# Two zero fills of a decode kernel, moved from SP's queue to four uneven DMAs of GpSimd

## The chip, the core and the metric

The kernel runs on one core of a Trainium2 chip. A core has five engines with instruction queues of their own: TensorE (PE) for matrix products, VectorE (DVE), ScalarE (ACT), GpSimd (POOL) and SyncE (SP), which here only issues transfers. Data move between HBM, the memory outside the core, and SBUF, the memory inside it with 128 partitions, by 16 DMA engines. SP, ACT and GpSimd each put their transfers on a queue of their own, and all queues are served by the same 16 DMA engines. One transfer is split over several of these engines; each of them adds one to a semaphore when its share has landed.

The metric is the device time of one execution in microseconds (us). Before the change the median of 3 runs is 809.98 us (809.77 to 810.98). The execution that was profiled took 810.97 us, and its span, from the first to the last instruction, is 808.1 us.

## The reference

One decode step of a layer, forward and backward: attention over the last W = 4096 of 32768 cached positions, then a gated feed-forward part, and the gradients of everything.

```python
x = A_x
h = x + _A_ref(_layernorm(x, axis=-1), A_k_cache, A_v_cache, A_wq, A_wo)
h2 = h + _B_ref(_layernorm(h, axis=-1), B_w_gate, B_w_up, B_w_down)
...
W = min(4096, max(256, Sk // 4))
k = jnp.repeat(k_cache[:, :, Sk - W:, :], rep, axis=1)
v = jnp.repeat(v_cache[:, :, Sk - W:, :], rep, axis=1)
...
_out, _vjp = jax.vjp(_f, A_x, A_k_cache, A_v_cache, A_wq, A_wo, B_w_gate, B_w_up, B_w_down)
_grads = _vjp(grad_out)
```

The gradients of the two caches have the caches' shape: 8 heads, 32768 positions, 256 values in bf16. Only the last 4096 positions of a head are touched by the step. The gradient of the other 28672 is zero, and these zeros have to be written: 2 caches x 8 heads x 14.7 MB, 235 MB in all.

## The kernel before

The kernel computes the eight groups of heads one after the other, first forwards (`scores` and `moments`, K and V of three to four groups held in SBUF), then the middle part (output projection, feed-forward part, its backward pass), then the eight groups backwards, each of which ends with two stores of 2 MB (L589), the last 4096 positions of its gradients. ACT's queue (`LD`) carries the loads after the first few, and all stores of results.

SP's queue (`ZQ`) carries the loads that come first: `x_bf` (L92), `wq` (L96, L97), K and V of the first groups, the gradient of the output and `wd` (L175 to L182). After these it does nothing but fill zeros, up to the end of the kernel. A fill writes one region of 2 MB: `zeros` is a tile of 128 partitions with ZW = 8192 bf16 values, 16 KB, in each. VectorE sets the first 5120 of its columns to zero and GpSimd the rest. The list `fills` holds the 112 regions in order: for each of the 8 heads 7 regions of `out_2` (the gradient of K) and 7 of `out_3` (of V). In memory a region is 128 rows of 16 KB that follow each other. One fill gives each of the 16 DMA engines 8 rows.

At most DEEP = 8 fills are in flight. Fill i counts on semaphore `zsem[i % 8]`, and SP waits for the fill eight places earlier before it issues the next (L195, in the profile under L196). After the last fill SP waits until all eight semaphores have their full count (L200 and L201). The fills are taken out of the planner's own bookkeeping, each with a semaphore of its own and in program order, and the last wait is declared as the fence for all of them. Nothing else in the kernel depends on a fill.

GpSimd has almost nothing to do: four constants, its part of `zeros` (L55) and two identity matrices. Its last instruction ends 4.2 us after the start. It issues no transfer.

Of the kernel before, what the change touches and what calls it, by code (L numbers as in the profile page):

```python
# [15 lines left out]
G = 8  # L16
Dh = 256
W = 4096
# [4 lines left out]
Sk = 32768  # L23
EPS = 1e-5
SCALE = 1.0 / 16.0
ZW = 8192
NZ = (Sk - W) * Dh // (128 * ZW)
ZM = 5120
DEEP = 8
# [5 lines left out]
def kernel(  # L35
        ctx, tc, A_x, A_k_cache, A_v_cache, A_wq, A_wo, B_x, B_w_gate, B_w_up, B_w_down, grad_out,
           out_0, out_1, out_2, out_3, out_4, out_5, out_6, out_7, out_8):
    nc = tc.nc
    LD = nc.scalar
    ZQ = nc.sync  # L40
# [12 lines left out]
    zeros = const.tile([128, ZW], bf16)  # L53
# [133 lines left out]
    fills = []  # L187
    for g in range(G):
        for o in (out_2, out_3):
            reg = o[0, g, 0:Sk - W, :].rearrange("s d -> (s d)").rearrange("(n p f) -> n p f", p=128, f=ZW)  # L190
            fills += [reg[i] for i in range(NZ)]
    zsem = [tc.alloc_semaphore(f"zsem{j}") for j in range(DEEP)]
    for i, reg in enumerate(fills):
        if i >= DEEP:
            tc.keep_in_program_order(ZQ.wait_ge(zsem[i % DEEP], 16 * (i // DEEP)))  # L195
        fill = ZQ.dma_start(out=reg, in_=zeros[:])  # L196
        tc.info.no_tile_sem_insts.add(fill.ins.name)
        tc.add_to_no_dep_group("fills", fill.ins)
        tc.keep_in_program_order(fill.then_inc(zsem[i % DEEP], 16))
    for j in range(DEEP):  # L200
        filled = tc.keep_in_program_order(ZQ.wait_ge(zsem[j], 16 * len(range(j, len(fills), DEEP))))  # L201
    tc.declare_fence(filled.ins, group="fills")
# [437 lines left out]
```

## Time and profile before

| what | value |
|---|---|
| median of 3 runs | 809.98 us |
| profiled execution, its time | 810.97 us |
| its span | 808.1 us |
| PE / DVE / ACT / POOL busy | 484.3 / 369.3 / 191.2 / 3.7 us |
| HBM read / written | 57.89 / 280.59 MB |
| fills on SP's queue | 112 x 2048 KB, 38.8 to 69.9 us from issue to landing, median 56.8 |
| stores of 2048 KB on ACT's queue (L589) | 16, median 17.4 us to landing |
| first fill issued | 17.9 us |
| ninth fill issued (the first that waits for a fill) | 58.06 us |
| last store of L589 issued | 727.6 us |
| last fill issued | 768.0 us |

Times within an execution are counted from the first instruction of the span. Views of the profile that are used below: the slices divide the span into 40 equal parts, and one digit is the busy share in tenths; a row of stretches begins with a stretch in us from the start and its length, then has the busy time and the number of instructions of PE, PEld, DVE, ACT and POOL, the clock granted to PE, the mean busy share of the 16 DMA engines and what they moved in GB/s; a line of the waits has the waiting engine with its line, what ended the wait, the us in total, the number of waits and the longest. A share slightly over 1 comes from packets that overlap by some ns.

### The profile page before, as it was taken

How to read it: one execution, taken by the hardware profiler on the slowest of the kernel's cores; microseconds unless marked ns; L12 is line 12 of the kernel's file. 1: busy time of each engine (PE TensorE's matmuls, PEld its weight loads, DVE VectorE, ACT ScalarE, POOL GpSimd, SP SyncE). 2: the span in 40 equal slices, each digit the busy share in tenths (PEclk: the TensorE clock that was granted, in tenths of full speed). 3: DMA queues.
4: the chain of work that ended last, by engine and by line, in shares of the span. 5: the costliest groups of instructions: out<-in, count | busy, mean ns of one | idle time of the engine just before them, and what ended most of it. 6: DMA issues, size and time to landing. Idle time of an engine off the chain costs nothing.

```text
span 808.1 us, 8346 instructions
## 1 busy us (share of the span) xinstructions
PE 484.3 (60%) x3128; PEld 252.7 (31%) x3151; DVE 369.3 (46%) x1152; ACT 191.2 (24%) x301; POOL 3.7 (0%) x9
## 2 busy tenths in 40 slices
PE   3799999999999955119326664533674664230000
PEld 2454545455455532108313322211231221000000
DVE  3279356455536417881336545258843444540000
ACT  1521331322330102001014243221232343330000
POOL 1000000000000000000000000000000000000000
PEclk9899999999999976559858557555555557555555
DMA  9999999999999999999999999999999999999994
GB/s 371 396 427 429 429 429 428 430 428 427 431 430 426 422 426 429 431 432 426 425 420 423 427 436 427 413 421 429 428 429 426 428 431 429 429 429 427 430 428 196
DMA packets 24942, 339.02 MB, mean 420 GB/s; under 512 B 2755, under 2 KB 3398, under 8 KB 4422
## 3 DMA queue, kind: packets, MB, share of 16 engines
q1 hardware_dynamic: 17842, 254.96, 74.4%
q10 hardware_dynamic: 7060, 83.53, 24.4%
q8 instruction: 24, 0.39, 0.2%
q14 instruction: 16, 0.13, 0.0%
HBM read 57.89 MB, written 280.59 MB: 419 GB/s over the span
## 4 chain that ended last, share of the span: by engine, by line
DMA 24%; PE 12%; DVE 11%; ACT 2%; issue 1%; DVEq 0%; ACTq 0%
DMA out_dram<-arena 24%; PE d_ps L579 4%; PE rows_ps L251 3%; PE tr_ps L248 3%; DVE arena L417 2%; DVE arena L587 2%; DVE arena L586 2%; DVE arena L472 1%; PE dqb_ps L458 1%; DVE arena L502 1%; DVE arena L595 1%; ACT arena L584 1%; ACT arena L539 1%; DVE arena L392 1%; ACT arena L583 0%
## 5 line engine op out<-in xcount | busy, mean ns | idle before, releaser
L579 PE MATMUL d_ps<-arena,rT 32*128 32x512 bf16 x256 | 59.5, 564 | 129.9 <-DVE arena L587 101.3
L303 DVE TENSOR_SCALAR arena<-arena,p_f 128x256 bf16<-128x256 bf16 x512 | 109.7, 281 | 53.8 <-PE M_ps L307 29.0
L248 PE MATMUL tr_ps<-ident_bf,arena 128*128 128x128 bf16 x1024 | 102.5, 254 | 29.1 <-DVE arena L541 25.4
L307 PE MATMUL M_ps<-arena 128*128 128x512 bf16 x489 | 118.4, 380 | 1.4 <-issue 0.6
L248 PEld LDWEIGHTS <-arena 128*128 128x128 bf16 x1024 | 74.5, 113 | 90.7 <-issue 88.6
L251 PE MATMUL rows_ps<-arena,vpad 128*16 128x512 bf16 x256 | 96.0, 470 | 6.0 <-ACT arena L265 2.8
L265 ACT COPY arena<-tr_ps 128x1024 bf16<-128x1024 bf16 x64 | 61.7, 1015 | 119.1 <-PE tr_ps L248 119.1
L587 DVE CAST arena<-d_ps 128x512 bf16<-128x512 f32 x64 | 43.5, 680 | 56.2 <-DMA out_dram<-arena 56.2
L583 ACT CAST arena<-d_ps 128x512 bf16<-128x512 f32 x64 | 37.7, 588 | 126.1 <-PE d_ps L579 122.2
L579 PEld LDWEIGHTS <-rT 32*128 32x128 bf16 x256 | 12.4, 98 | 165.2 <-issue 83.5
L307 PEld LDWEIGHTS <-arena 128*128 128x128 bf16 x512 | 46.4, 98 | 52.3 <-issue 6.3
L586 DVE CAST arena<-d_ps 128x512 bf16<-128x512 f32 x64 | 44.0, 688 | 37.4 <-PE d_ps L579 37.3
L311 PE MATMUL ok_ps<-arena 128*16 128x256 bf16 x512 | 59.3, 273 | 1.1 <-DVE arena L292 0.9
L584 ACT CAST arena<-d_ps 128x512 bf16<-128x512 f32 x64 | 38.1, 595 | 64.4 <-DMA out_dram<-arena 64.4
L311 PEld LDWEIGHTS <-arena 128*16 128x16 bf16 x512 | 44.5, 90 | 14.7 <-issue 4.5
L539 ACT COPY arena<-tr_ps 128x1024 bf16<-128x1024 bf16 x32 | 32.8, 1026 | 16.0 <-PE tr_ps L248 11.9
L251 PEld LDWEIGHTS <-vpad 128*16 128x16 bf16 x256 | 17.8, 91 | 44.1 <-issue 37.4
L541 DVE COPY arena<-tr_ps 128x1024 bf16<-128x1024 bf16 x32 | 21.9, 685 | 13.5 <-PE tr_ps L248 12.7
L463 ACT ACTIVATE arena<-dqb_ps 128x512 bf16<-128x512 f32 x8 | 4.8, 597 | 79.9 <-PE dqb_ps L461 55.0
L458 PE MATMUL dqb_ps<-arena,doT_f 128*128 128x256 f32 x64 | 19.5, 435 | 4.7 <-ACT arena L463 4.7
L417 DVE CUSTOM_DVE_ANT_0 arena<-arena,dh_bc 128x448 bf16<-128x448 bf16 x32 | 20.0, 624 | 1.1
L253 DVE COPY arena<-rows_ps 16x512 f32<-16x512 f32 x16 | 10.8, 675 | 19.9 <-PE rows_ps L251 19.7
(182 smaller groups left out, 318.1 us busy)
## 6 DMA issues: line engine op xcount, KB each, us to landing
out_dram<-zeros SPq DMA_DIRECT2D x112, 2048.0 KB, 56.8
out_dram<-arena ACTq DMA_DIRECT2D x16, 2048.0 KB, 17.4
arena<-in_A_v_cache_dram ACTq DMA_DIRECT2D x8, 2048.0 KB, 14.8
arena<-in_A_k_cache_dram ACTq DMA_DIRECT2D x5, 2048.0 KB, 21.2
arena<-in_A_v_cache_dram SPq DMA_DIRECT2D x4, 2048.0 KB, 30.5
arena<-in_A_k_cache_dram SPq DMA_DIRECT2D x3, 2048.0 KB, 26.1
arena<-in_A_wo_dram ACTq DMA_DIRECT2D x1, 3584.0 KB, 19.3
arena<-in_A_wq_dram SPq DMA_DIRECT2D x1, 3072.0 KB, 10.2
```

What stands on the lines that cost most here:

```text
L248: nc.tensor.transpose(tr_ps[:, dh, i, :], X_sb[:, 4 * q + i, dh * 128:(dh + 1) * 128], ident_bf[:])
L251: nc.tensor.matmul(rows_ps[:], lhsT=pad[:, dh, 16 * q:16 * q + 16], rhs=XT[:, dh].rearrange("p t k -> p (t k)"), start=(q == 0 and dh == 0 ...
L265: sT_ps = dots(K_slot[g % 3], KT_slot, vpad[g % 2], rows1, ps_c, "cols", lambda q, XT, ps: nc.scalar.copy(out=XT, in_=ps))
L303: nc.vector.tensor_scalar(out=pK[:, i, hh, :], in0=K_sb[:, t, :], scalar1=p_f[:, 8 * i + c, hh:hh + 1], scalar2=None, op0=ALU.mult)
L307: nc.tensor.matmul(M_ps[:, vh, :], lhsT=V_sb[:, t, vh * 128:(vh + 1) * 128], rhs=pK[:, i, :, :].rearrange("p h d -> p (h d)"), start=(t == ...
L311: nc.tensor.matmul(ok_ps[:, k, :], lhsT=ppad[g % 2][:, 8 * (t % 4) + t // 4, :], rhs=X_sb[:, t, :], start=(g == 0 and k == 0 and t == 0), ...
L539: nc.scalar.copy(out=XT, in_=ps)
L579: nc.tensor.matmul(d_ps[:, qi].rearrange("p w d -> p (w d)"), lhsT=rT[32 * q:32 * (q + 1), :], rhs=RB_[32 * q:32 * (q + 1), l, :], start=T ...
L583: nc.scalar.copy(out=stV[:, t:t + 2, :], in_=d_ps[:, :, 0, :])
L584: nc.scalar.copy(out=stK[:, t:t + 2, :], in_=d_ps[:, :, 1, :])
L586: nc.vector.tensor_copy(out=stV[:, t:t + 2, :], in_=d_ps[:, :, 0, :])
L587: nc.vector.tensor_copy(out=stK[:, t:t + 2, :], in_=d_ps[:, :, 1, :])
```

## The change

The last two regions of `out_3` of the last head are taken from the list of SP's fills. They lie behind each other in memory: 256 rows of 16 KB, `last`. GpSimd writes them in four DMAs, each with a semaphore of its own, after it has waited for the first of SP's fills:

- rows 0 to 67, 4 times 17 rows, read from partitions 0, 4, 8 and 12 of `zeros`, each of them 17 times over
- row 68 without its last element, read from partition 16
- rows 69 to 119, 3 times 17 rows, read from partitions 20, 24 and 28
- rows 120 to 255, 8 times 17 rows, read from partitions 64, 68 and so on up to 92

The last element of row 68 is written by SP, as a DMA of one element ahead of its first fill. The row without it has 8191 elements, which is a prime. SP then issues 110 fills as before, and waits for the five new semaphores before it waits for the eight old ones. The helper `fill_with` holds the three lines that every fill had.

```diff
+    def fill_with(queue, dst, src, sem):
+        fill = queue.dma_start(out=dst, in_=src)
+        tc.info.no_tile_sem_insts.add(fill.ins.name)
+        tc.add_to_no_dep_group("fills", fill.ins)
+        tc.keep_in_program_order(fill.then_inc(sem, 16))
+
+    last = out_3[0, G - 1, 0:Sk - W, :].rearrange("s d -> (s d)").rearrange("(r f) -> r f", f=ZW)[(NZ - 2) * 128:NZ * 128]
+    tc.keep_in_program_order(nc.gpsimd.wait_ge(zsem[0], 16))
+    psem = []
+
+    def share(queue, dst, src):
+        psem.append(tc.alloc_semaphore(f"psem{len(psem)}"))
+        fill_with(queue, dst, src, psem[-1])
+
+    for r0, k, p0 in ((0, 4, 0), (68, 0, 16), (69, 3, 20), (120, 8, 64)):
+        if k:
+            share(nc.gpsimd, last[r0:r0 + 17 * k].rearrange("(k n) f -> k n f", n=17), zeros[p0:p0 + 4 * k:4].unsqueeze(1).to_broadcast([k, 17, ZW]))
+        else:
+            share(nc.gpsimd, last[r0:r0 + 1, 0:ZW - 1], zeros[p0:p0 + 1, 0:ZW - 1])
+    share(ZQ, last[68:69, ZW - 1:ZW], zeros[0:1, 0:1])
+
+    fills = fills[:-2]
     for i, reg in enumerate(fills):
         if i >= DEEP:
             tc.keep_in_program_order(ZQ.wait_ge(zsem[i % DEEP], 16 * (i // DEEP)))
-        fill = ZQ.dma_start(out=reg, in_=zeros[:])
-        tc.info.no_tile_sem_insts.add(fill.ins.name)
-        tc.add_to_no_dep_group("fills", fill.ins)
-        tc.keep_in_program_order(fill.then_inc(zsem[i % DEEP], 16))
+        fill_with(ZQ, reg, zeros[:], zsem[i % DEEP])
+    for sem in psem:
+        tc.keep_in_program_order(ZQ.wait_ge(sem, 16))
     for j in range(DEEP):
         filled = tc.keep_in_program_order(ZQ.wait_ge(zsem[j], 16 * len(range(j, len(fills), DEEP))))
```

## The prediction

> **What bounds the kernel now.** I read the page's slices first, then its queues, then stretches of the end, and last the packets of the end one by one.
>
> ```profile
> DMA  9999999999999999999999999999999999999994
> GB/s 371 396 427 429 429 429 428 430 428 427 431 430 426 422 426 429 431 432 426 425 420 423 427 436 427 413 421 429 428 429 426 428 431 429 429 429 427 430 428 196
> ...
> q1 hardware_dynamic: 17842, 254.96, 74.4%
> q10 hardware_dynamic: 7060, 83.53, 24.4%
> ```
>
> The sixteen DMA engines are busy from the first slice to the last but one, at about 428 GB/s, and 339 MB have to pass. q1 is SP's queue (all zero fills and the first loads), q10 is ACT's. So the time is what the DMA engines have to carry, and no compute engine sets it. Only the last slice (20.2 us long) is half empty. Stretches of it, with the DMA share in the last column but one:
>
> ```profile
> 727.00:751.00 24.00, 0.00 (x0) 0.00 (x0) 0.21 (x1) 0.60 (x2) 0.00 (x0) 0.50 1.01 428
> ...
> 768.00:792.00 24.00, 0.00 (x0) 0.00 (x0) 0.00 (x0) 0.00 (x0) 0.00 (x0) 0.50 1.01 429
> 792.00:794.00 2.00, 0.00 (x0) 0.00 (x0) 0.00 (x0) 0.00 (x0) 0.00 (x0) 0.50 0.88 377
> 794.00:796.00 2.00, 0.00 (x0) 0.00 (x0) 0.00 (x0) 0.00 (x0) 0.00 (x0) 0.50 0.69 295
> 796.00:798.00 2.00, 0.00 (x0) 0.00 (x0) 0.00 (x0) 0.00 (x0) 0.00 (x0) 0.50 0.56 238
> 798.00:800.00 2.00, 0.00 (x0) 0.00 (x0) 0.00 (x0) 0.00 (x0) 0.00 (x0) 0.50 0.23 98
> 800.00:802.00 2.00, 0.00 (x0) 0.00 (x0) 0.00 (x0) 0.00 (x0) 0.00 (x0) 0.50 0.08 33
> 802.00:804.00 2.00, 0.00 (x0) 0.00 (x0) 0.00 (x0) 0.00 (x0) 0.00 (x0) 0.50 0.08 33
> 804.00:806.00 2.00, 0.00 (x0) 0.00 (x0) 0.00 (x0) 0.00 (x0) 0.00 (x0) 0.50 0.06 25
> ```
>
> From 728 us on nothing computes; until 792 all engines copy zeros; then they run out one after the other. A share of 0.06 is one engine of sixteen: from 801.5 us on a single engine works. The view of the DMA queues from there:
>
> ```profile
> DMA packets 10, 0.13 MB, mean 20 GB/s; under 512 B 2, under 2 KB 2, under 8 KB 2
> ```
>
> Eight packets of 16 KB and two of 4 bytes (the count on the semaphore): this engine's whole last fill, while the other fifteen have nothing. SP waits for it:
>
> ```profile
> SPq L201 <- DMA out_dram<-zeros: 38.4, 4, 23.9
> ```
>
> The records of the packets (queue, start, length, size; no engine number) can be followed, since an engine starts a packet 3 to 4 ns before its last one ends. In the end the sixteen chains finish at 792.4, 793.2, 793.9, 794.9, 795.4, 795.4, 797.3, 797.6, 797.7, 797.9, 798.2, 799.1, 799.3, 799.9, 800.7 and **806.4 us**. Mean 797.5, median 797.6: one engine is 8.8 us late against the median and 5.7 against the next. In the same chains, where they can be followed, the late engine carries 9 of the 16 packets of 8 KB of the instruction queue q14 (0.31 us each, 2.8 us), and its 16 KB packets take 619 ns in the mean against 615 (4 ns by 1,152 packets, 4.6 us). I take both to come back in every execution, and the lateness as a property of one engine and not as chance.
>
> **The change, part by part.** The price of a row (16 KB) is the step between packets of the late engine in its last fill: 801.536 to 802.143, 0.607 us.
>
> *Taken off.* Two fills leave SP: 2 x 8 = 16 rows on each engine, 16 x 0.607 = 9.7 us on each.
>
> *Added, if the four parts fall as the change means them, on engines 0 to 3, 4, 5 to 7 and 8 to 15.* 68/4, 51/3 and 136/8 are 17 rows on fifteen engines, 10.3 us, and one row on engine 4, 0.6 us. Net: fifteen engines +0.61 us, engine 4 -15 x 0.607 = -9.1 us. If engine 4 is the late one, it ends at 806.4 - 9.1 = 797.3 us, and the end is set by the next: 800.7 + 0.6 = 801.3. **Gain 806.4 - 801.3 = 5.1 us.**
>
> *The price of a row issued by GpSimd* is not in the trace. Lower bound: 0.607, the row of SP's own; a 4 KB packet of the load of L97 steps by 0.153 to 0.155, four of them 0.61 to 0.62, so cutting the rows would cost nothing either. Upper bound: the 16 KB packets of the instruction queue q8, from another ring, at about 0.94 us in the records: 17 x (0.94 - 0.607) = 5.7 us on fifteen engines, which eats the gain (801.3 + 5.7 = 807.0, 0.6 later than before). It is a copy of zeros out of SBUF like SP's, so I take 0.607.
>
> *Which engine gets which rows* decides the sum, and no row of GpSimd's DMAs is there to read. [...]
>
> *Issue.* GpSimd's last instruction before the change ends at 4.2 us; its four DMAs hold up nobody behind them. They wait for the first fill's semaphore, which SP's ninth fill also waits for (issued at 58.06 us), so they start there and have until 801 to land. Should an issue take even tens of us, 740 us cover it.
>
> *SP's one-element DMA* stands before the first fill (17.9 us) and delays it and all behind it by one issue: 0.33 us (the median of L196's issues), or nothing if the loads still in the rings cover it. The stretch 20 to 30 us has a DMA share of 0.90, so some of the delay can become empty time: I take +0.2, bounds 0 and 0.33.
>
> *SP's four new waits and the fifth for the one element* stand after the last fill and before the eight old ones. The shares landed some 700 us earlier; behind them queue only those eight waits, of which the longest lasts 23.9 us today. Nothing.
>
> *Three rings in place of two from 58 us.* Until GpSimd's 17 rows are through (17 x 0.607 x 2 to 3 rings = 21 to 31 us) ACT's loads get a third of an engine and not half. The loads of K and V issued at 68.5 and 70.5 us land in 14.2 to 22.6 us today (all four from 60 to 110 us); by 3/2 that is 21 to 34, and the groups follow each other every 30 us, so PE may stall some 4 us once. What hides it: the last store is issued at 727.6 and landed by 751, and 55 us of nothing but fills follow. Without this cover it would cost these 4 us.
>
> *Sum:* -5.1 + 0.2 = **-4.9 us**. Against the profiled execution (span 808.1, its time 810.97) that is 806.1; the median of the runs is 809.98, 1.0 lower, so I put the forecast at **805.1 us**, -0.6%. Its own range goes from 803.4 (the next engine 1.7 us earlier than in this execution; the five before it lie within 2.5) to 807.0 (a third of the upper surcharge for GpSimd's rows, 1.9 us).
>
> **Rivals.** *The late engine is not the one relieved.* The records give no number. Against it: the relief, 9.7 us relative to the others, is the size of the lateness, 8.8; and the one-packet transfers of 896 bytes lie on chains that are not late, so at least the engine that takes single packets is not meant. For it: nothing else in the trace marks engine 4. Then the late engine gets its extra row: +0.6 + 0.2, 809.98 + 0.8 = 810.8 us. [...] No run here has shown a number so far.
>
> *The parts are not what they say.* If each is spread over all sixteen engines, or the row of 8,191 elements is cut, nobody is relieved: 809.98 + 0.2 = 810.2 us.
>
> *The parts pile up on the first engines, slower.* If every part starts at engine 0 with one partition to an engine, engine 0 gets 17 + 1 + 17 + 17 = 52 rows in place of 16. It becomes the end as soon as its surplus passes its lead: (806.4 - 797.5)/0.607 = 15 rows; here it is 36, 21.9 us. From the mean 797.5 that ends at 819.4, 13.0 us later than now: 809.98 + 13.0 + 0.2 = **823.2 us**. For it: the diff names partitions and counts, no engine, and a DMA that is told nothing else may start at the first. Against it: nothing in the trace. [...]
>
> *The row is as dear as q8's packets:* the end is at 807.0, 0.6 later than now: 809.98 + 0.6 + 0.2 = 810.8 us.
>
> **How the numbers follow.** Forecast 0.60; late engine elsewhere 0.18; spread evenly 0.05; dear rows 0.03; piled up 0.14. The first is faster, the next three lie within 0.2% (1.6 us, about what a measurement of this kernel can tell from no change), the last is slower: faster 0.60, same 0.26, slower 0.14. The range reaches from 803.4 to 811.2, over forecast and the cases of no change, and leaves the pile-up out.
>
> **What would show it.** Right: a queue of GpSimd with 256 packets of 16 KB, 4.19 MB; the stretch with a share of 0.06 gone and the share falling from full to nothing within about 9 us and not 14; SP's longest wait behind the last fill shorter by about 5 us; 1.01 up to about 793. Wrong: a lone engine that still copies a whole fill at the end (not the one relieved), one that copies for over 10 us alone (piled up), packets of GpSimd well over 0.62 us. The prediction fails above all if the number 4 is not the late engine's.

## The result and the profile after

The changed kernel takes 815.07 us (median of 5 runs, 813.7 to 817.01) against 809.98 us before (median of 5, 809.74 to 810.98): 0.6% slower, a ratio of 1.0062 with a 95% interval of [1.0045, 1.0079]. The forecast was 805.1 us, the range ended at 811.2. The profiled execution took 813.7 us with a span of 811.9.

The slices and the new queue on the page of the changed kernel:

```profile
DMA  9999999999999999999999999999999999999996
GB/s 369 398 427 428 395 354 396 430 424 429 424 431 427 416 424 429 434 429 430 427 420 427 425 430 429 415 418 429 432 428 425 429 432 427 434 428 430 430 428 265
...
q0 software_dynamic: 896, 4.20, 1.5%
```

q0 is GpSimd's queue: 256 packets of data, 4.20 MB as planned, and 640 packets of 4 bytes. The row of DMA digits shows nothing, but the rate falls to 395, 354 and 396 GB/s in the fifth to seventh slice, where 429, 429 and 428 stood. The same in stretches of 20 us (the last three columns are PE's clock, DMA share and GB/s):

```profile
60.00:80.00 20.00, 20.00 (x115) 9.90 (x114) 18.36 (x92) 3.00 (x4) 1.59 (x3) 1.00 1.01 426
80.00:100.00 20.00, 19.87 (x146) 10.54 (x145) 6.49 (x31) 7.51 (x12) 0.00 (x0) 1.00 1.01 402
100.00:120.00 20.00, 16.98 (x97) 8.72 (x95) 10.60 (x50) 2.61 (x3) 0.00 (x0) 0.83 1.00 352
120.00:140.00 20.00, 19.87 (x152) 11.33 (x151) 7.68 (x35) 6.73 (x12) 0.00 (x0) 1.00 1.01 400
```

A share of 1.00 at 352 GB/s means that the engines are always at work on a packet and that the packets take longer. The whole stretch from 60 to 160 us, first in the kernel before and then in this one:

```profile
60.00:160.00 100.00, 98.75 (x656) 51.51 (x666) 57.06 (x269) 29.18 (x44) 0.00 (x0) 1.00 1.01 429
60.00:160.00 100.00, 96.59 (x627) 49.28 (x625) 54.29 (x253) 27.56 (x38) 1.59 (x3) 0.97 1.01 400
```

So 100 x 29/429 = 6.8 us of all engines is lost there. From 60 to 80 us, where the first of GpSimd's parts runs, the rate is 426 GB/s against 430 before; the loss comes with the later parts. One sign that the prediction had named as "wrong" is there: packets of GpSimd well over 0.62 us. Its rows take 764 ns in the mean. The end:

```profile
798.00:800.00 2.00, 0.00 (x0) 0.00 (x0) 0.00 (x0) 0.00 (x0) 0.00 (x0) 0.50 0.85 360
800.00:802.00 2.00, 0.00 (x0) 0.00 (x0) 0.00 (x0) 0.00 (x0) 0.00 (x0) 0.50 0.73 311
802.00:804.00 2.00, 0.00 (x0) 0.00 (x0) 0.00 (x0) 0.00 (x0) 0.00 (x0) 0.50 0.69 295
804.00:806.00 2.00, 0.00 (x0) 0.00 (x0) 0.00 (x0) 0.00 (x0) 0.00 (x0) 0.50 0.48 205
806.00:808.00 2.00, 0.00 (x0) 0.00 (x0) 0.00 (x0) 0.00 (x0) 0.00 (x0) 0.50 0.25 106
808.00:810.00 2.00, 0.00 (x0) 0.00 (x0) 0.00 (x0) 0.00 (x0) 0.00 (x0) 0.50 0.10 41
```

All engines end later: the share is under 0.5 from 804 us on, before from 798 on, and the last fill is complete at 810.1 us against 806.4. One sign that the prediction had named as "right" came true all the same, in SP's waits behind its last fill:

```profile
SPq L222 <- DMA out_dram<-zeros: 38.4, 5, 19.1
```

The longest is 4.8 us shorter (23.9 before). With 110 fills in place of 112 another fill is the first that is waited for; this number follows the order of the waits and says nothing of the late engine.

When the packets are followed from engine to engine as in the prediction, the row of 16,382 bytes (at 88.87 us, 1.16 us long) stands on an engine that has done its 17 rows of the *first* part. No engine has a single row alone, and one has none. So the theory for the experiments: the row took no engine of its own and did not move the place at which the next DMA starts. The three shares fell on engines 4 to 6 and the eight on 7 to 14, each one engine lower than meant. Then engine 4 has 17 rows and is not relieved. Engines are numbered here in the order in which GpSimd's DMAs take them; the trace has no numbers. The sources in the diff suppose that partition 0 goes with engine 0, 4 with engine 1 and so on to 28 with engine 7, and 64 to 92 with engines 8 to 15; these are called an engine's own partitions below. If SP's fills are split in this way, each of these eleven engines reads from the partitions that the engine above it reads in the fills. The rival: the parts lie where they should, and GpSimd's rows are dear by themselves.

### The profile page after: what moved, and what is told of

It reads as the page before. It is cut to its first block, busy times and chain, and to the rows that moved or that the text cites. A ratio compares the mean times of both kernels' runs of the same rounds, so it can differ in the third digit from the quotient of the medians.

```text
span 811.9 us, 8375 instructions
## 1 busy us (share of the span) xinstructions
PE 487.9 (60%) x3151; PEld 253.0 (31%) x3151; DVE 369.5 (46%) x1152; ACT 191.2 (24%) x301; POOL 6.5 (1%) x13
## 5 line engine op out<-in xcount | busy, mean ns | idle before, releaser
L328 PE MATMUL M_ps<-arena 128*128 128x512 bf16 x512 | 123.2, 385 | 0.0
L616 DVE CUSTOM_DVE_ANT_0 arena<-arena 128x4096 bf16<-128x4096 bf16 x3 | 13.3, 4421 | 14.9 <-DMA arena<-in_A_wq_dram 14.9
## 6 DMA issues: line engine op xcount, KB each, us to landing
arena<-in_A_v_cache_dram ACTq DMA_DIRECT2D x8, 2048.0 KB, 19.4
arena<-in_A_k_cache_dram ACTq DMA_DIRECT2D x5, 2048.0 KB, 23.3
arena<-in_A_wq_dram SPq DMA_DIRECT2D x1, 3072.0 KB, 10.5
```

The source lines that it names most:

```text
L328: nc.tensor.matmul(M_ps[:, vh, :], lhsT=V_sb[:, t, vh * 128:(vh + 1) * 128], rhs=pK[:, i, :, :].rearrange("p h d -> p (h d)"), start=(t == ...
```

## The experiments

All times are medians beside runs of the kernel before on the same chip, whose medians were 809.85 to 810.28 us.

**Sources moved to where the theory has the shares.** Only partitions change:

```diff
-    for r0, k, p0 in ((0, 4, 0), (68, 0, 16), (69, 3, 20), (120, 8, 64)):
+    for r0, k, p0 in ((0, 4, 0), (68, 0, 0), (69, 3, 16), (120, 8, 60)):
```

> The changed kernel with other source partitions for three of GpSimd's four DMAs, nothing else: the row of 8191 from partition 0, the three shares from 16, 20, 24, the eight shares from 60, 64, ... 88. [...] With these sources every engine reads its own: GpSimd's rows take 0.61 us, the stretch from 80 to 135 us keeps about 428 GB/s (changed kernel: 339 to 410), and the time is 810.6 to 811.0 us, since the late engine keeps one row more than before (+0.6). Rival (dear rows: GpSimd's rows slow everything whatever they read): about 815 us as in the changed kernel. [...]

Measured: 811.58 us (810.67 to 812.35, 11 runs), ratio 1.0015 [1.0007, 1.0024]: 3.5 us under the changed kernel, and still 0.6 over the 811.0 us expected at most. DMA queues in the changed kernel from 80 to 110 us (packets, MB, share of 16 engines' time):

```profile
q1 hardware_dynamic: 383, 5.57, 50.1%
q10 hardware_dynamic: 248, 3.54, 27.6%
q0 software_dynamic: 386, 2.29, 23.3%
```

and the same stretch with the sources moved:

```profile
q1 hardware_dynamic: 431, 6.24, 48.8%
q10 hardware_dynamic: 277, 4.01, 31.3%
q0 software_dynamic: 430, 2.59, 20.8%
```

23.3% of 480 us is 111.8 us for 2.29 MB, 140 rows: 0.80 us a row, the small packets included. With the sources moved it is 20.8%, 99.8 us for 158 rows, 0.63 us. SP's rows gain as well (0.71 to 0.62 us by the same sum). The same bytes to the same addresses by the same engines: where a row is *read* makes the difference. That it comes from two readers of the same partitions, and not from the distance, agrees with the changed kernel from 60 to 134 us, where the chains can be followed. Engine 15 has no row of GpSimd's, but engine 14 reads from its partitions, and its own 16 KB packets take 730 ns in the mean. Engines 0 to 3, whose partitions no other engine reads, have 618 to 624 ns. If the parts had lain where the change meant them, this edit would have put them wrong and made things worse.

**Aligned and turned, without the odd row.** Three parts of 4, 4 and 8 engines with 16 rows each, no relief; first from the partitions of their own engines, then each from those of the next:

```diff
-    for r0, k, p0 in ((0, 4, 0), (68, 0, 16), (69, 3, 20), (120, 8, 64)):
...
+    for r0, k, p0 in ((0, 4, 0), (64, 4, 16), (128, 8, 64)):    # aligned
+    for r0, k, p0 in ((0, 4, 4), (64, 4, 20), (128, 8, 68)):    # turned
+        share(nc.gpsimd, last[r0:r0 + 16 * k].rearrange("(k n) f -> k n f", n=16), zeros[p0:p0 + 4 * k - 3:4].unsqueeze(1).to_broadcast([k, 16, ZW]))
```

> The two fills by GpSimd in three even parts, 4, 4 and 8 engines with 16 rows each, read from partitions 0 to 12, 16 to 28 and 64 to 92, no one-row DMA: nobody is relieved. [...] Rival (dear rows): 6 us of all engines are lost again, about 815 to 816 us.

> [...] Rival (dear rows): the same time as the even kernel within 0.2%.

Measured: aligned 810.56 us (809.95 to 811.46, 11 runs), ratio 1.0005 [0.9996, 1.0013], just over the 809.9 to 810.5 us expected if nothing is lost; turned 819.52 us (817.14 to 821.22, 4 runs), 1.012 [1.0105, 1.0136], inside the 816 to 820 us expected if the partitions make the difference. The stretch from 60 to 160 us, aligned:

```profile
60.00:160.00 100.00, 99.61 (x672) 52.05 (x671) 57.06 (x269) 29.18 (x44) 1.06 (x2) 1.00 1.01 424
```

and turned:

```profile
60.00:160.00 100.00, 92.59 (x611) 48.08 (x609) 52.06 (x245) 26.72 (x38) 0.96 (x2) 0.95 1.00 396
```

So reading each share from the next engine's partitions costs 28 GB/s over 100 us, and 9 us in all. A row of GpSimd's took 0.78 us from 60 to 110 us, against 0.64 aligned, by the sum used above (20.7% and 18.2% of 800 us, for 3.48 and 3.74 MB, the small packets included). The fills of GpSimd by themselves cost about 1 us at most (the upper end of the aligned interval). The two runs agree with the assignment that the diff's sources suppose; no trace shows it directly.

**Engine 4 given almost nothing, first try.** Six DMAs of half rows; the three small ones have one piece to an engine. They are to leave engine 4 one row and give each of the others 17:

```diff
+    for k, n, p0 in ((4, 33, 0), (4, 1, 16), (8, 1, 64), (5, 1, 0), (3, 33, 20), (8, 33, 64)):
```

> [...] If engine 4 is the late one: 805.1 us, 0.6% faster. Theory (the late engine lies among engines 1 to 3, since in the changed kernel the chain with the instruction queue q14 carried rows of the first part): 810.6 to 811.0 us, the late engine has one row more. Dear rows: 815 us or more.

Measured: 813.66 us (813.43 to 815.51), ratio 1.0045 [1.0032, 1.0058]. None of the three numbers was met, for a reason that is itself an answer. In the chains, engines 0 to 3 have their 33 half rows and then three single ones: each DMA with one piece to an engine began at the first engine, and none moved the place for the next. So the large parts behind them fell on 4 to 6 and 7 to 14 again, with the source partitions of others, and the rate from 60 to 160 us was 404 GB/s.

**Which engine is late?** With 16 pieces of 512 bytes to an engine for the small parts the place does move, by the rates below. First engine 2 is left one row, then engine 3, and the others have 17:

```diff
+    for k, n, w, p0 in ((2, 33, 4096, 0), (6, 16, 256, 8), (8, 16, 256, 64), (3, 16, 256, 0), (5, 33, 4096, 12), (8, 33, 4096, 64)):    # engine 2
+    for k, n, w, p0 in ((3, 33, 4096, 0), (5, 16, 256, 12), (8, 16, 256, 64), (4, 16, 256, 0), (4, 33, 4096, 16), (8, 33, 4096, 64)):    # engine 3
```

> [...] If engine 2 is the late one the time is 805.1 to 806 us; if not, 810.6 to 811.2. [...]

> The same for engine 3: 3 engines with 33 half rows, 5 and 8 with pieces of 512 bytes, 4 with pieces, 4 and 8 with 33 half rows. [...] If neither this nor the kernel for engine 2 is faster and both are free of slow rows, engine 1 is left of the three, or the lateness does not belong to one engine.

Measured: 811.49 us (810.93 to 812.68), 1.0017 [1.0008, 1.0026], and 811.36 us (810.88 to 812.92), 1.0016 [1.0007, 1.0025], both 0.2 to 0.3 over the 810.6 to 811.2 us expected for "not the late one". From 60 to 160 us the rates are 422 and 423 GB/s, as in the kernels whose shares are read from their own engines' partitions (422 and 424). With engine 3 relieved the end is:

```profile
802.00:804.00 2.00, 0.00 (x0) 0.00 (x0) 0.00 (x0) 0.00 (x0) 0.00 (x0) 0.50 0.06 25
804.00:806.00 2.00, 0.00 (x0) 0.00 (x0) 0.00 (x0) 0.00 (x0) 0.00 (x0) 0.50 0.08 33
806.00:808.00 2.00, 0.00 (x0) 0.00 (x0) 0.00 (x0) 0.00 (x0) 0.00 (x0) 0.50 0.04 16
```

One engine still works alone for 5 us. And the engine that carries most of q14's packets is the one without rows here, and ended at 792.4 us: it is number 3, and not the late one.

Then a kernel, run once, whose fourteen parts make each engine known: eight pairs of engines, then groups of 3, 2, 3, 3, 2 and 3, each with 8 rows, issued after SP's 96th fill. For each part without rows for it an engine handles 9 small packets, and one behind each set of its own (1,760 in all, of the 2,016 packets of its queue). So the numbers of small packets before, between and behind an engine's two sets of rows tell which it is:

```diff
-    tc.keep_in_program_order(nc.gpsimd.wait_ge(zsem[0], 16))
+    tc.keep_in_program_order(nc.gpsimd.wait_ge(zsem[7], 16 * 12))
...
+    for k, n, p0 in ((2, 8, 0), (2, 8, 8), (2, 8, 16), (2, 8, 24), (2, 8, 64), (2, 8, 72), (2, 8, 80), (2, 8, 88), (3, 8, 0), (2, 8, 12), (3, 8, 20), (3, 8, 64), (2, 8, 76), (3, 8, 84)):
```

> A look, not a gain: which engine is the late one. Neither engine 2 nor engine 3 is, by the two kernels before: in both a lone engine still ended some 5 us behind the rest while the relieved one stopped early. [...] The place of an engine's rows among the counts on the semaphores tells its number, and from there to the end its packets can be followed without a gap. Theory (one and the same engine is late): the lone engine of the last 5 us is again there, at about 806 us, it is none of 2, 3 and 15, and it has 8 + 8 rows like all others. Rival (no engine is late as such; whichever has the last of the fills by chance): the lone engine is any, 3 among them. Time 809.9 to 810.6 us.

Measured: 811.56 us, 1.0 over the range. When the sixteen chains are followed back from their ends, the one that ends alone, at 807 us, has 18 small packets, 8 rows, 55 small packets, 8 rows and 37 small packets. That is engine 4: two parts before (18), six between (54 + 1), four behind (36 + 1). The chain with 18, 64 and 28, which is engine 5, ends at 799.9 us, and the one with 9, 64 and 37, engine 3, at 802.1 us. The late engine is number 4, as the change has it.

**Engine 4 relieved, and the change with its row altered.** The first of the two kernels leaves engine 4 16 KB, about one row, and gives each of the others 17.

```diff
+    for k, n, w, p0 in ((4, 33, 4096, 0), (4, 16, 256, 16), (8, 16, 256, 64), (5, 16, 256, 0), (3, 33, 4096, 20), (8, 33, 4096, 64)):
```

> The 4.19 MB in six DMAs of GpSimd, all of them with several pieces per engine, so that the place of the next engine moves on with each: 4 engines x 33 pieces of 8 KB, 4 x 16 pieces of 512 B, 8 x 16 of 512 B, 5 x 16 of 512 B, 3 x 33 of 8 KB, 8 x 33 of 8 KB. [...] Theory (the late engine is number 4, and what ate the gain was the row that took no engine of its own): the lone engine at the end is gone, the share falls from full to nothing within 9 us, and the time is 805.1 to 806.5 us (-5 us for the engine, up to +1 for what all kernels with DMAs of GpSimd lost). Rival (the late engine is another, or lateness follows the load rather than an engine): 810.6 to 811.8 us, with one engine that ends alone near 807. Rival (relief of one engine shows in the tail, but the DMAs of GpSimd cost what is won): lone end gone, 808 to 810 us.

```diff
-            share(nc.gpsimd, last[r0:r0 + 1, 0:ZW - 1], zeros[p0:p0 + 1, 0:ZW - 1])
-    share(ZQ, last[68:69, ZW - 1:ZW], zeros[0:1, 0:1])
+            share(nc.gpsimd, last[r0:r0 + 1, 0:17 * 481].rearrange("k (n f) -> k n f", n=17), zeros[p0:p0 + 1, 0:481].unsqueeze(1).to_broadcast([1, 17, 481]))
+    share(ZQ, last[68:69, 17 * 481:ZW], zeros[0:1, 17 * 481:ZW])
```

> The change with one thing altered: row 68 is written by GpSimd as 17 pieces of 481 elements from partition 16, where the change has one piece of 8,191 elements, and its last 15 elements (in place of one) by SP. [...] Rival (a DMA with one partition stays at the first engine whatever its pieces): the shares shift by one as in the change, rows of 0.73 to 0.87 us at 80 to 110 us, 813 to 815.5 us.

Measured: with engine 4 relieved 807.44 us (806.29 to 810.32, 12 runs), ratio 0.997 [0.9961, 0.9978], the first of the kernels faster than before; above the 805.1 to 806.5 of the theory, below its rivals' 808. The lone engine at the end is gone:

```profile
800.00:802.00 2.00, 0.00 (x0) 0.00 (x0) 0.00 (x0) 0.00 (x0) 0.00 (x0) 0.50 0.27 115
802.00:804.00 2.00, 0.00 (x0) 0.00 (x0) 0.00 (x0) 0.00 (x0) 0.00 (x0) 0.50 0.06 25
804.00:806.00 2.00, 0.00 (x0) 0.00 (x0) 0.00 (x0) 0.00 (x0) 0.00 (x0) 0.50 0.00 0
```

With the row in 17 pieces 813.79 us (813.4 to 816.32), 1.0053 [1.0041, 1.0066]: inside the 813 to 815.5 us of the rival. The 17 pieces of 962 bytes were spread, two each over eight engines (8 packets of 1,924 bytes) and one on a ninth (a packet of 966 bytes), and the place again did not move. So several pieces did not move it where all lie in one partition. The prediction's pile-up rival has every part start at engine 0; that held for the smallest of the change's parts alone.

**Engine 3 too, and later.** Five DMAs with larger pieces, which leave engine 4 half a row, engine 3 10.5 and the others 17.5; then the same after SP's 88th fill:

```diff
+    for k, n, w, p0 in ((3, 8, 7680, 0), (2, 4, 1024, 12), (3, 20, 7168, 20), (8, 20, 7168, 64), (4, 10, 8192, 0)):
...
-    tc.keep_in_program_order(nc.gpsimd.wait_ge(zsem[0], 16))
+    tc.keep_in_program_order(nc.gpsimd.wait_ge(zsem[7], 16 * 11))    # later
```

> As x8_engine4, but engines 3 and 4 are both relieved, in five DMAs of GpSimd: 3 engines x 8 pieces of 15 KB, 2 x 4 pieces of 2 KB, 3 x 20 of 14 KB, 8 x 20 of 14 KB, 4 x 10 of 16 KB. [...] Fewer packets of 4 bytes too (some 750 after 1,185). Rival (the last engine of x8_engine4 is any of the fourteen, which now get half a row more): 807.4 to 808.0 us.

> x10_two with GpSimd's DMAs issued later, after SP's 88th fill in place of the first, so that they share the engines at some 690 to 750 us and not at 60 to 140 us. Theory (what all kernels with GpSimd's DMAs still lose is lost where three queues meet while the loads of K and V run; late, few loads are left): 0.3 to 1.0 us less than x10_two. Rival (the loss is the packets of 4 bytes and the sharing itself, wherever they stand): the same as x10_two within 0.3 us.

Measured: 807.62 us (805.98 to 808.49, 5 runs), 0.9964 [0.9953, 0.9976], and later 805.91 us (803.62 to 807.07, 6 runs), 0.9946 [0.9934, 0.9958]. Early, the relief of engine 3 brought nothing over the kernel with engine 4 alone relieved, as the rival said. Late was 1.7 us better, more than the 0.3 to 1.0 of the theory, and the two intervals overlap a little.

**The changed kernel and the relieved one, both issued late** (the edit of the wait alone):

> The changed kernel with one thing altered: GpSimd waits for SP's 88th fill in place of the first, so its four DMAs run at some 665 to 740 us, with few loads left. [...]

> x8_engine4 with GpSimd's DMAs issued after SP's 88th fill as in x12_late. [...] Theory (807.4 of x8_engine4 holds 1.5 to 2 us of early loss, the relief of engine 4 by itself is worth what the chains of the kernel before show, 5.1 less 0.2): 805.1 to 806.2 us. Rival (relieving engine 3 as well was what made x12_late faster): 806.8 to 807.6 us.

Measured: 813.56 us (813.25 to 814.91), 1.005 [1.0038, 1.0063], and 807.18 us (806.16 to 807.98), 0.9965 [0.9954, 0.9977]. Issued late, the changed kernel still loses most of what it loses early, inside the 813 to 815.5 us expected if the sources alone make its rows slow; 810.3 to 811.5 us was expected if it takes the loads of K and V too. So the loss does not need these loads. The stretch from 660 to 760 us, first in the kernel before and then in it:

```profile
660.00:760.00 100.00, 28.51 (x170) 10.37 (x168) 33.30 (x67) 26.41 (x46) 0.00 (x0) 0.55 1.01 429
660.00:760.00 100.00, 28.78 (x174) 10.40 (x173) 34.11 (x69) 26.31 (x46) 2.59 (x4) 0.55 1.00 407
```

That is 22 GB/s less, where it was 29 early. The kernel with engine 4 relieved gained nothing clear from being late (807.44 early), and lies inside its rival's range. The same stretch of it has:

```profile
660.00:760.00 100.00, 26.99 (x161) 9.69 (x159) 32.30 (x65) 25.45 (x45) 4.06 (x6) 0.55 1.01 422
```

That is 7 GB/s less, 1.6 us of 100: still a loss, with every row read from the engine's own partitions.

**Fewer and larger pieces.** The last kernel is the late one with engine 3 not relieved, to tell whether that or the pieces made the difference:

```diff
-    for k, n, w, p0 in ((3, 8, 7680, 0), (2, 4, 1024, 12), (3, 20, 7168, 20), (8, 20, 7168, 64), (4, 10, 8192, 0)):
+    for k, n, w, p0 in ((3, 4, 1024, 0), (2, 4, 1024, 12), (3, 17, 8192, 20), (8, 17, 8192, 64), (4, 19, 7168, 0)):
```

> As x12_late, but engine 3 is not relieved: 3 engines x 4 pieces of 2 KB, 2 x 4 of 2 KB, 3 x 17 of 16 KB, 8 x 17 of 16 KB, 4 x 19 of 14 KB, on engines 0-2, 3-4, 5-7, 8-15, 0-3: engine 4 gets half a row, the others some 17.1 rows, nearly all in pieces of 14 and 16 KB, after SP's 88th fill. Theory A (x12_late was faster than x14_engine4_late for its fewer and larger pieces): 805.6 to 806.4 us, the mean rate of 660 to 760 us at 425 GB/s or more as in x12_late. Theory B (it was the relief of engine 3): 806.8 to 807.6 us, the rate at 425 and yet the last chain ending at 802 to 803.

Measured: 806.08 us (805.01 to 806.25, 5 runs), ratio 0.9944 [0.9931, 0.9958]. That is theory A: it was the pieces, 1.1 us against the late kernel with engine 4 relieved, though the two intervals overlap a little. Piece size and number of small packets changed together, and no run tells them apart. Its stretch of copying and its end:

```profile
660.00:760.00 100.00, 25.71 (x157) 9.02 (x156) 31.91 (x65) 25.24 (x44) 3.17 (x5) 0.55 1.01 427
...
796.00:798.00 2.00, 0.00 (x0) 0.00 (x0) 0.00 (x0) 0.00 (x0) 0.00 (x0) 0.50 0.69 295
798.00:800.00 2.00, 0.00 (x0) 0.00 (x0) 0.00 (x0) 0.00 (x0) 0.00 (x0) 0.50 0.31 131
800.00:802.00 2.00, 0.00 (x0) 0.00 (x0) 0.00 (x0) 0.00 (x0) 0.00 (x0) 0.50 0.08 33
802.00:804.00 2.00, 0.00 (x0) 0.00 (x0) 0.00 (x0) 0.00 (x0) 0.00 (x0) 0.50 0.00 0
```

427 GB/s, and the share falls to nothing within some 10 us with the last fill complete at 801.98 us: the end that the prediction drew, at 801.3, for a change that would do what it says. This kernel and the late one with both engines relieved are the fastest measured, each 4.2 us under the kernel before in its own comparison.

## Why the prediction was wrong

- *The DMA engines bound the kernel, and one late engine sets the end.* Right; every run that left the late engine with its rows ended with a lone engine or later than before.
- *The late engine is number 4.* Right, by the kernel with fourteen parts, and by the three places tried: 811.49 with engine 2 relieved, 811.36 with engine 3, 807.44 with engine 4. In part this was luck. That it is number 4 was taken from the change, whose relief is about as large as the lateness, and the two reasons given for its being late in every execution do not hold. Most packets of q14 go to engine 3, which is not the late one once two chains that cross are kept apart. And when the chains are kept apart, the late engine's rows take 615 ns in the mean, where those of the others lie between 613 and 620. By the landings of SP's fills in the kernel before, the last of the sixteen shares trails their median by 1.2 us at 57 us, 5.4 at 238, 10.3 at 427, 15.9 at 738 and 9 from 764 us on. What makes engine 4 late stays open.
- *Relief is worth 5.1 us.* Right in size where the pieces are large and issued late: the last fill was foretold to end at 801.3 us and ended at 801.98, and the time fell by 4.2 us (4.9 foretold for the sum). The other kernels with engine 4 relieved fell by 2.4 (early), 2.5 (early, engine 3 too), 2.8 (late) and 4.2 us (late, engine 3 too). None has the change's whole rows at the change's early time.
- ***Which engine gets which rows* is the step that failed.** The sum has the parts on engines 0 to 3, 4, 5 to 7 and 8 to 15, and no run shows the changed kernel's parts there. In its chains they lie on 0 to 3, 4 to 6 and 7 to 14; the part of one row took no step: it was put on an engine of the first part, and the place stayed at 4. The shares slid by one, so engine 4 kept its load and got 17 rows in place of one, and eleven engines read partitions of a neighbour: 3.5 us, by the run that only moved the sources. That this choice decides the sum was said; that the *source* of a row has a price that depends on the engine was not, although the diff's partitions (20, 24, 28 and 64 to 92) are chosen engine by engine.
- *A row of GpSimd's costs 0.607 us, at most 0.94.* Right when it is read from the engine's own partitions: in the last kernel 10.3% of 1,600 us from 660 to 760 us is 164.8 us for 4.20 MB, 256 rows, and less 719 small packets of some 9 ns that is 0.62 us a row. In the changed kernel it was 0.80 us in the worst 30 us, inside the bounds, and not its row alone: SP's rows beside it rose from 0.62 to 0.71. The prediction raised only the 17 rows by its upper price.
- *Three queues delay loads, and the end covers it.* Right in the main. The four loads of K and V from 60 to 110 us landed in 19.4 to 36.5 us (21 to 34 foretold; the slow rows are in this too). From 82 to 90 us the queues of SP, ACT and GpSimd had 95, 96 and 96 packets; in the kernel before, from 72 to 80 us, those of SP and ACT had 107 and 108. PE stood idle for 3.0 us from 100 to 110 us; the engines had nothing left to compute from 740 us on while the fills ran to 810, so no stall of PE reached the end.
- *SP's one-element DMA, +0.2 us, and the new waits, nothing.* No run singles out a cost: none differs in the element alone.
- *The rivals.* Pile-up on the first engines was the only one well slower; it happened to one row and not to the parts. That nobody is relieved was priced at 810.2 us, for another reason. A slide by one place, with rows read from a neighbour's partitions, was not among them.

The forecast missed by 815.07 - 805.1 = 10.0 us. By the medians, 811.58 - 806.08 = 5.5 of them is the relief that did not happen (the kernel with its sources moved, without relief, against the last one with it). These two differ in the time of issue and the pieces as well; against the early kernel with engine 4 relieved it is 4.1. The neighbours' partitions are 815.07 - 811.58 = 3.5, and 806.08 - 805.1 = 1.0 is left. The last may be what GpSimd's DMAs cost even when all is right; no run shows it by itself.

Open is why the kernel with engines 3 and 4 relieved early ends with a lone engine (last fill at 804.9 us, its neighbour at 801.9) and the same kernel issued late does not (800.6). Their rates while GpSimd's DMAs run, 425 and 426 GB/s, don't explain 1.7 us.

## What to carry to other kernels

When a DMA is meant for certain engines, find out from one run where its packets went before anything is built on it, above all for parts with a single row or piece. Where the DMA engines are the bound, a share of 1.0 is not enough: read the rate beside it, since an engine whose packets are slow counts as busy: 1.00 stood beside 352 GB/s here. And before a tail is balanced over engines, ask from which partitions each engine reads: 9 us lay between two kernels that differ in that alone.

## What the runs showed of the hardware that was not expected

- Rows were slow where two DMA engines read the same SBUF partitions, by the assignment that the diff's sources suppose: 0.78 us for a 16 KB row of GpSimd in place of 0.64 (the turned and the aligned kernel, 60 to 110 us, small packets included), packets up to 1,955 ns in the changed kernel, 730 ns for the own packets of an engine whose partitions another one reads, and 28 GB/s less for the whole core over 100 us. Read from the engine's own partitions a row from GpSimd cost what SP's does (0.62 us in the last kernel; 613 to 620 ns by engine in the kernel before).
- In these runs a DMA of GpSimd with one contiguous piece for each partition started at the first engine and left the place for the next one where it was (one row; four, eight and five half rows). So did one with 17 pieces of a single partition, which were dealt two to an engine. One with several pieces for each of k partitions took the next k engines (k = 2, 3, 4, 5, 6 and 8).
- In these runs a DMA for k engines occupied the others too: for n pieces to an engine each engine without data handled n + 1 packets of 4 bytes, and one with data a single one: 640 in the changed kernel (12 x 18 + 4, 15 x 2 + 1, 13 x 18 + 3, 8 x 18 + 8), some 9 ns each. Pieces of 512 bytes shared packets, eight to one of 4,096 bytes, and an engine without data had 32 bytes in its place. With 1,247 small packets (62 of them of 32 bytes) and 8 KB pieces the late relieved kernel had 422 GB/s from 660 to 760 us; with 719 and mostly 16 KB pieces 427.
